# Pooled attention and a top-1 mixture of experts: four instead of two early slots, their tokens turned by way of a DRAM scratch, and one table for all later slots

## The chip, the cores and the metric

The kernel runs on one core of a Trainium2 chip. The metric is device microseconds for one execution. A core has TensorE (PE in the profile: matmuls and transposes), VectorE (DVE), ScalarE (ACT), GpSimd (POOL, which also issues the gathers and scatters) and SyncE (SP, which issues the plain DMAs). Each works through its own instructions in order, and semaphores make them wait for one another.

## The reference

```python
# q, k, v: [8, 8, 576, 64]; attention over keys and values averaged in groups of 8
k_p = k.reshape(B, H, Sp, 8, D).mean(axis=3)
v_p = v.reshape(B, H, Sp, 8, D).mean(axis=3)
scores = scale * np.matmul(q, k_p.transpose(0, 1, 3, 2))
attn = softmax(scores)
x = np.matmul(attn, v_p)                   # as [4608 tokens, 512]
# each token goes to one of 8 experts
logits = x @ w_gate + modality_bias[modality_id]
e_idx = np.argmax(logits, axis=1)
gate_w = probs[np.arange(N), e_idx]        # softmax of the logits, at the chosen expert
for e in range(E):
    mask = e_idx == e
    h = np.maximum(x[mask] @ w1[e], 0.0)   # 512 -> 1024
    out[mask] = gate_w[mask, None] * (h @ w2[e])   # 1024 -> 512
```

## The kernel before

**Two stages.** Attention runs in 20 steps (lines 980 to 1062), each over up to 256 tokens. Its results go to a DRAM buffer `xs`, one row of 528 numbers a token: 512 values, the gate weight in column 512 and eight factors. The expert stage then runs over slots of 256 tokens of one expert (`part`, line 1303). There are 18 full slots of tokens, and a few more are needed because each expert's last slot is only partly filled.

**Slots.** For each slot, GpSimd gathers its rows of `xs` into `xg` (line 144), the tokens are brought from [token, feature] to [feature, token], and split into a high and a low part (`xhl`) for matmuls in fp32r. The first layer is `first_pair` (line 204): two of eight blocks of 128 hidden units at a time, eight matmuls of 512 columns (line 209) and eight of 256 (line 214). Behind them ScalarE copies half of the sums (line 217), VectorE adds the other (line 218), and the results are split again (lines 221 and 223). The second layer is `second` (line 1337), six matmuls a block. `pairs` (line 1377) runs one slot so: the first layer of a pair, then the second layer of the pair before it. At a slot's end `next_pair` starts the first pair of the next slot, for which that slot's `xhl` must be complete, both parts of both tiles of 128 tokens.

**Slot 0** is shorter. Its first layer (`first0`, line 227) runs among the last steps of attention, so that `slot0` (line 1451) has eight calls of `second`, with `next_pair` of slot 1 ahead of the last one.

**Early slots.** Slots 0 to EARLY_SLOTS - 1 hold tokens of the first expert (that of the first token) out of the first half of the tokens alone (T_EARLY tiles), so that they can be listed before attention is done. `early_table` (line 841) makes their index table `gidx0`: VectorE operations on line 868, one for each of 2 x EARLY_SLOTS columns, two on line 870, 18 matmuls (line 860), and five small operations (lines 834 to 838), behind which the gathers are issued. The operations of this table and of the routing of a group of tokens (`route`, line 731) are a list, `drip`. `gap(n)` (line 546) issues up to n of them in the gaps of VectorE's attention work, but stops at a *held* one, which has matmuls. A held one is issued by `release` at the start of a step (line 995), and only if it stood at the head of the list when line 1055 looked, in the step before:

```python
            due = bool(drip) and drip[0] in held        # line 1055, behind hook_2 of a step
```

The early table enters the list in step 11, behind the routing of the second group; the third group's routing enters in step 16, behind the table. Slot 0's tokens are turned by TensorE at the end of step 17 (line 921).

**Two ways to turn tokens.** `x_transposes` (line 167) uses eight matmuls of TensorE (line 173) for a slot's two tiles, a copy of ScalarE (line 175) and a subtraction of VectorE (line 176). Slots from FIRST_BLOCKED = 3 go another way ("blocked"): `blocks_out` (line 1251) has VectorE multiply by the factors into an order of 32 x 32 blocks, and SP writes each tile to a DRAM scratch `scr`; `blocks_in` (line 1266) reads it back in four transfers a tile; `blocks_turn` (line 1276) has VectorE transpose the blocks; `blocks_high` (ScalarE) and `blocks_low` (VectorE) split. `misc` (line 1410) places these: out in the slot before the one before at f = 4 and 5, in two blocks later, turn, high and low in the slot before at f = 2 to 5. Here `f` is the block of the slot in hand.

**Tables for later slots.** After the last group's routing, `late` (line 1212) places counts, bases, expert numbers, and two tables (`table`, line 1132): six columns (slots 2 to 4) in slots 0 and 1, and 44 columns (the rest) in slots 1 and 2. Each has 36 matmuls (line 1142) and three wide VectorE operations (lines 1144 and 1147). Weights are loaded by SP under a condition (`load_w`), only where a slot's expert differs from the one before; after slot 0 the first expert's weights are loaded again without a condition, because the raw tiles had been used otherwise.

Of the kernel before, what the change touches and what calls it, by code (L numbers as in the profile page):

```python
# [25 lines left out]
EARLY_SLOTS = 2  # L26
EXTRA = (128,)
QUAD = 32
FIRST_BLOCKED = 3
# [4 lines left out]
def kernel(  # L34
# [114 lines left out]
    def gather(s, idx, col, xgs, rows=NTOK):  # L149
        for tt in range(2):  # L150
            gather_tile(xgs[(2 * s + tt) % 4], idx, col + tt, rows)
# [52 lines left out]
    def first_pair(f, ab, between=lambda: None, mid=lambda: None):  # L204
# [6 lines left out]
        mid()  # L211
# [27 lines left out]
    with ExitStack() as actx:  # L239
# [601 lines left out]
        def early_table():  # L841
# [31 lines left out]
            ops += [lambda: [gather(s, gidx0, 2 * s, xg, T_EARLY * P) for s in range(EARLY_SLOTS)]]  # L873
# [286 lines left out]
    def row(a):  # L1160
# [9 lines left out]
        lambda: load_regs(EARLY_SLOTS, meta[0:1, 1 + EARLY_SLOTS:2 + EARLY_SLOTS], None),  # L1170
# [26 lines left out]
    for i, r in enumerate(EXTRA):  # L1197
# [13 lines left out]
    first_cols = table(c4, c4 + 6)  # L1211
# [36 lines left out]
    def gate_of(s, tt):  # L1248
        return gc[:, 2 * s + tt:2 * s + tt + 1] if s >= EARLY_SLOTS - 1 else xg[(2 * s + tt) % 4][:, D:D + 1]

    def blocks_out(s, tt):

        x = xg[(2 * s + tt) % 4] if tt < 2 else xe
        to = xg[(2 * s + 2 + tt % 2) % 4][:, 0:D] if s > FIRST_BLOCKED else ye[:, (4 + tt) * D:(5 + tt) * D]
        xp = to.rearrange("p (j k r) -> p j k r", j=NQ, r=QUAD)
        f = x[:, RX:RX + H].rearrange("p (k a o q) -> p k a o q", a=2, o=1, q=1)
        for a in range(2):
            nc.vector.tensor_tensor(
                xp[:, 2 * a:2 * a + 2].rearrange("p j k r -> p k j r"),
                x[:, 0:D].rearrange("p (k a j r) -> p a k j r", k=ND, a=2, j=2)[:, a],  # L1260
                f[:, :, a].to_broadcast([P, ND, 2, QUAD]), op=ALU.mult)
# [4 lines left out]
    def blocks_in(s, tt):  # L1266
        n = len(tts_of(s))
        if tt == 0 and s <= FIRST_BLOCKED + 1:
# [7 lines left out]
    def blocks_turn(s, tt):  # L1276
        if s <= FIRST_BLOCKED + 1:
# [25 lines left out]
    def part(s):  # L1303
# [49 lines left out]
        def renew(f):  # L1353
# [297 lines left out]
```

## Time and profile before

| | |
|---|---|
| median of 3 runs | 593.76 us (591.69 to 594.55) |
| the profiled execution's own time | 590.98 us |
| its span, first to last instruction | 589.3 us |
| TensorE busy | 570.9 us, 97% of the span |
| VectorE, ScalarE, GpSimd busy | 372.7, 273.8, 187.2 us |
| mean granted clock of TensorE | 0.998 |
| DMA | 92.60 MB, mean 157 GB/s |

A row of a timeline has the start in us from the span's start, the time from the first to the last of the instructions that it merges, engine, line, operation, tiles and shapes, and in brackets the idle time of the engine before it and what ended that. The chain of work that ended last has start, length and what. A row of stretches has the stretch, its length, busy time and number of instructions of PE, PEld (weight loads), DVE, ACT and POOL, the granted clock, the DMA engines' busy share and GB/s. SPq and the like is the issuing of DMAs by that engine.

### The profile page before, as it was taken

The page shows a single profiled execution, that of the slowest core. Times are in us where ns is not written, and L with a number is a line of the kernel's source. Part 1 is how long each engine was busy: PE and PEld are TensorE (multiplying, and loading weights), DVE is VectorE, ACT ScalarE, POOL GpSimd, SP SyncE. Part 2 cuts the span into 40 slices and gives each one's busy share as a digit, 9 for nine tenths or more (in the row PEclk, how much of TensorE's full clock was granted, in tenths as well). Part 3 has the DMA queues.
Part 4 walks back from the last instruction along what each step waited for, and adds up shares of the span by engine and source line. Part 5 has one row for each costly group of instructions (what it writes and reads, how often), then busy time and mean ns, then how long its engine had stood idle before and what let it go on. Part 6 is the DMA issues. An engine that isn't in the chain of part 4 may idle for free.

```text
span 589.3 us, 12333 instructions
## 1 busy us (share of the span) xinstructions
PE 570.9 (97%) x3539; PEld 499.6 (85%) x3539; DVE 372.7 (63%) x945; ACT 273.8 (46%) x652; POOL 187.2 (32%) x290
## 2 busy tenths in 40 slices
PE   6999999999999999999999999999999999999995
PEld 5789789988898888888888888888888888888894
DVE  5877898788966766557455446855455487555311
ACT  2767677788552333333333336633333474334210
POOL 7679967765000323112112102112102113212101
PEclk9999999999999999999999999999999999999999
DMA  8999979995311744232232277242234843241101
GB/s 257 306 323 282 360 219 309 304 313 171 103 54 39 263 169 121 79 125 91 82 118 95 86 230 241 91 125 91 87 111 137 255 158 105 91 146 54 38 3 55
DMA packets 83426, 92.60 MB, mean 157 GB/s; under 512 B 17871, under 2 KB 58319, under 8 KB 83344
## 3 DMA queue, kind: packets, MB, share of 16 engines
q1 hardware_dynamic: 77424, 72.24, 39.2%
q0 software_dynamic: 5920, 19.44, 9.9%
q8 instruction: 30, 0.49, 0.4%
q14 instruction: 52, 0.43, 0.2%
HBM read 123.06 MB, written 27.58 MB: 256 GB/s over the span
## 4 chain that ended last, share of the span: by engine, by line
PE 82%; DVE 7%; DMA 5%; ACT 2%; issue 1%; SPq 1%; POOLq 0%; POOL 0%; DVEq 0%; ACTq 0%
PE op L1345 33%; PE hp L209 20%; PE hp L214 10%; PE av L667 4%; PE hp L183 3%; PE sc L603 3%; DMA q<-in_q_dram 3%; PE av L671 2%; DMA v<-in_v_dram 2%; PE pp L632 2%; PE pq L578 2%; PE ph L183 1%; DVE mx L610 1%; DVE hl L141 1%; DMA out_dram<-obw,slw 1%
## 5 line engine op out<-in xcount | busy, mean ns | idle before, releaser
L209 PE MATMUL hp<-xhl,hl 128*128 128x512 f32 x512 | 126.6, 390 | 0.0
L1321 POOL DMA_INDIRECT out_dram<-ob,sidx x34 | 36.8, 1083 | 263.6 <-DVE ob L1315 191.2
L209 PEld LDWEIGHTS hp<-xhl,hl 128*128 128x128 f32 x512 | 96.1, 188 | 19.9
L217 ACT COPY ht<-hp 128x256 f32<-128x256 f32 x128 | 47.3, 373 | 138.7 <-PE hp L214 112.3
L218 DVE TENSOR_TENSOR ht<-ht,hp 128x256 f32<-128x256 f32 x128 | 52.8, 420 | 92.5 <-ACT ht L217 89.4
L1345 PE MATMUL op<-hl,hx 128*128 128x512 f32 x429 | 104.8, 392 | 0.0
L1345 PEld LDWEIGHTS op<-hl,hx 128*128 128x128 f32 x429 | 78.5, 189 | 14.6
L1345 PE MATMUL op<-hl,hh 128*128 128x512 f32 x256 | 79.8, 393 | 0.0
L214 PEld LDWEIGHTS hp<-xhl,hl 128*128 128x128 f32 x512 | 69.8, 191 | 4.9
L214 PE MATMUL hp<-xhl,hl 128*128 128x256 f32 x512 | 71.5, 283 | 0.0
L1345 PEld LDWEIGHTS op<-hl,hh 128*128 128x128 f32 x256 | 46.0, 189 | 7.8
L667 PE MATMUL av<-vw,pt 128*128 128x146 f32 (+1 forms) x320 | 49.2, 293 | 1.4 <-DVE xb L700 1.3
L1345 PE MATMUL op<-hl,hlo 128*128 128x512 f32 x128 | 49.9, 390 | 0.0
L144 POOL DMA_INDIRECT xg<-xs,gidx x36 | 38.6, 1073 | 29.0 <-DMA raw<-in_moe_w_dram 13.8
L667 PEld LDWEIGHTS av<-vw,pt 128*128 128x128 f32 (+1 forms) x320 | 39.6, 180 | 3.4 <-DVE xb L700 1.0
L223 DVE SCALAR_TENSOR_TENSOR hx<-ht,hx 128x256 fp32r<-128x256 f32 x64 | 27.2, 427 | 18.8 <-DVEq L1350 15.7
L223 DVE SCALAR_TENSOR_TENSOR hlo<-ht,hh 128x256 fp32r<-128x256 f32 x64 | 27.1, 425 | 18.5 <-DVEq L1350 15.3
L603 PE MATMUL sc<-kt,qt 128*128 128x144 f32 x256 | 37.4, 289 | 0.6 <-DVE rs L798 0.3
L603 PEld LDWEIGHTS sc<-kt,qt 128*128 128x128 f32 x256 | 33.2, 190 | 1.6 <-DVE rs L798 0.5
L610 DVE TENSOR_REDUCE mx<-sc 128x8 f32<-128x576 f32 (+1 forms) x40 | 27.7, 692 | 7.5 <-PE sc L603 6.9
L671 PE MATMUL av<-vw,pt 128*128 128x146 f32 (+1 forms) x160 | 30.0, 290 | 0.0
L221 ACT ACTIVATE hx<-ht 128x256 fp32r<-128x256 f32 x64 | 26.2, 419 | 7.4 <-DVE ht L218 5.7
(279 smaller groups left out, 907.7 us busy)
## 6 DMA issues: line engine op xcount, KB each, us to landing
raw<-in_moe_w_dram SPq DMA_DIRECT2D x288, 256.0 KB
xs<-xb SPq DMA_DIRECT2D x16, 528.0 KB
scr<-xg SPq DMA_DIRECT2D x29, 256.0 KB
k<-in_k_dram SPq DMA_DIRECT2D x7, 1024.0 KB
v<-in_v_dram SPq DMA_DIRECT2D x7, 1024.0 KB
q<-in_q_dram SPq DMA_DIRECT2D x7, 1024.0 KB
y<-scr SPq DMA_DIRECT2D x108, 64.0 KB
v<-in_v_dram SPq DMA_DIRECT2D x16, 128.0 KB
```

What stands on the lines that cost most here:

```text
L144: nc.gpsimd.indirect_dma_start(out=x, out_offset=None, in_=xs[0:rows, :], in_offset=IndirectOffsetOnAxis(idx[:, col:col + 1].bitcast(U32), 0),
L209: nc.tensor.matmul(hp[g % 2], hl[g][:, 0, d * P:(d + 1) * P], ab[:, d, :, 0:SLOT], start=(d == 0), stop=False)
L214: nc.tensor.matmul(hp[g % 2][:, 0:SLOT], hl[g][:, 1, d * P:(d + 1) * P], ab[:, d, 0, 0:SLOT], start=False, stop=(d == ND - 1))
L217: nc.scalar.copy(hts[g % 2], hp[g % 2][:, SLOT:2 * SLOT])
L218: nc.vector.tensor_add(hts[g % 2], hts[g % 2], hp[g % 2][:, 0:SLOT])
L223: nc.vector.scalar_tensor_tensor(hlo, hts[g % 2], 0.0, hh.bitcast(F32), op0=ALU.max, op1=ALU.subtract)
L603: nc.tensor.matmul(dst, qt[:, i, :], kt[b % NB][:, :, h * SPL:(h + 1) * SPL], start=True, stop=True)
L610: nc.vector.reduce_max(mx, scv, axis=AX.X)
L667: nc.tensor.matmul(av[hs, u, 2 * VC * gg:2 * VC * (gg + 1)], pt[:, c, hs], vw[y][:, c].rearrange("p a x -> p (a x)"), start=(gg == 0), sto ...
L671: nc.tensor.matmul(dst4[hs], pt4[:, hs], v4[y][:, 2 * u:2 * u + 2, :], start=False, stop=True)
L1321: nc.gpsimd.indirect_dma_start(out=out[:, :], out_offset=IndirectOffsetOnAxis(idx.bitcast(U32), 0), in_=ob, in_offset=None, bounds_check=N ...
L1345: nc.tensor.matmul(ot, l[:, ts_], hl[f][:, w, D:2 * D], start=(f == 0 and n == 0), stop=(f == NF - 1 and n == 2))
```

## The change

EARLY_SLOTS goes from 2 to 4 and FIRST_BLOCKED from 3 to 1. So four slots are filled from the first half's tokens, and the early table has eight columns. Slots 1 to 3 (the second to the fourth) go through the scratch as well. For the early ones the factors are 1, and ScalarE copies into block order in place of VectorE's multiplication. Slot 1's tokens are sent out and read back ahead of slot 0's first `second`, and turned and split in slot 0 at f = 3 to 6. `x_transposes` is left for slot 0 and for slots past the full ones. The two later tables become one of 50 columns (NSLOT goes from 27 to 29), with its VectorE work in slot 1 and its matmuls at the start of slot 2; counts and bases move from f = 3 to f = 2 of slot 0. The weights' reload moves from the end of slot 0 to slot 2 and becomes conditional. Gate weights are always kept in `gc`.

```diff
-EARLY_SLOTS = 2
+EARLY_SLOTS = 4
-FIRST_BLOCKED = 3
+FIRST_BLOCKED = 1
...
-    first_cols = table(c4, c4 + 6)
+    t = table(c4, NCOL, 4)
     late = {
         (0, 0): [lr[9], lr[7], lr[11], lr[8]],
         (0, 1): [lr[10]],
-        (0, 3): [counts, lr[12]] + [fn for pair in zip(bases, lr[13:20]) for fn in pair] + lr[20:25],
-        (0, 4): experts,
-        (0, 5): lr[25:] + columns,
-        (0, 6): first_cols[:3],
-        (1, 0): first_cols[3:] + changes,
+        (0, 2): [counts, lr[12]] + [fn for pair in zip(bases, lr[13:20]) for fn in pair] + [lr[20]],
+        (0, 6): lr[21:24],
+        (0, 7): lr[24:27],
+        (1, 0): lr[27:],
+        (1, 2): experts,
+        (1, 3): columns,
+        (1, 4): changes,
+        (1, 5): t[0:1],
+        (1, 6): t[1:2],
+        (1, 7): t[2:3],
+        (2, 0): t[3:5],
+        (2, 1): t[5:7],
+        (2, 2): t[7:],
     }
...
-    t = table(c4 + 6, NCOL, 4)
-    for i, at_ in enumerate(((1, 3), (1, 7), (2, 1), (2, 3), (2, 4), (2, 5), (2, 6))):
-        late[at_] = t[i:i + 1]
-    late[2, 7] = t[7:]
...
-        to = xg[(2 * s + 2 + tt % 2) % 4][:, 0:D] if s > FIRST_BLOCKED else ye[:, (4 + tt) * D:(5 + tt) * D]
+        to = xg[(2 * s + 2 + tt % 2) % 4][:, 0:D]
...
+            if s < EARLY_SLOTS:
+                nc.scalar.copy(xo, xi)
+            else:
+                nc.vector.tensor_tensor(xo, xi, f[:, :, a].to_broadcast([P, ND, 2, QUAD]), op=ALU.mult)
...
-                if nxt2 and s + 2 > EARLY_SLOTS:
+                if nxt2 and s + 2 == EARLY_SLOTS:
+                    new_raw(f)
+                if nxt2 and s + 2 >= EARLY_SLOTS:
                     load_w(s + 2, f)
...
-                    turn = g == NF - 2 and not blocked(s + 1)
-                    first_pair(g, tokens_of(s), pop, (lambda: x_transposes(s + 1, xg)) if turn else (lambda: None))
+                    first_pair(g, tokens_of(s), pop)
...
-            if f == (3 if s < EARLY_SLOTS else 2) and blocked(s + 2):
-                gather(s + 2, gidx, 2 * (s + 2), xg)
+            if f == 2 and blocked(s + 2):
+                gather(s + 2, xg)
...
                 for tt in tts_of(s + 1):
-                    if f == 4 + tt:
+                    at_ = f - tt - (0 if s else 1)
+                    if at_ == 4:
                         blocks_low(s + 1, tt)
...
                 second(f)
-                renew(f)
-                if f == 4:
-                    x_transposes(s + 1, xg)
                 do_late(s, f)
-            for f in range(NF):
-                new_raw(f)
-                load_w(EARLY_SLOTS, f)
+                misc(f, [])
...
+    for tt in range(2):
+        keep_gate(0, tt, nc.gpsimd)
+        blocks_out(1, tt)
+    for tt in range(2):
+        blocks_in(1, tt)
     for s in range(NSTAT - 1):
         parts[s][0](tail)
```

More of the change, by code (lines that the diff above doesn't have):

```diff
@@ L147, in gather_tile, with gather @@
             bounds_check=rows - 1, oob_is_err=False)
-    def gather(s, idx, col, xgs, rows=NTOK):
+    def gather(s, xgs):
         for tt in range(2):
-            gather_tile(xgs[(2 * s + tt) % 4], idx, col + tt, rows)
+            gather_tile(xgs[(2 * s + tt) % 4], gidx0 if s < EARLY_SLOTS else gidx, 2 * s + tt,
+                        T_EARLY * P if s < EARLY_SLOTS else NTOK)
     def scale_tile(x):
@@ L202, in first_wide, with first_pair @@
         nc.vector.scalar_tensor_tensor(hlo, t, 0.0, hh.bitcast(F32), op0=ALU.max, op1=ALU.subtract)
-    def first_pair(f, ab, between=lambda: None, mid=lambda: None):
+    def first_pair(f, ab, between=lambda: None):
         fs = (f, f + 1)
@@ L210, in first_pair @@
                                  start=(d == 0), stop=False)
-        mid()
         for g in fs:
@@ L872, in early_table @@
             ops += finish_table(lambda: psm["t"], C, gidx0, sidx0, "t0")
-            ops += [lambda: [gather(s, gidx0, 2 * s, xg, T_EARLY * P) for s in range(EARLY_SLOTS)]]
+            ops += [lambda: [gather(s, xg) for s in range(2)]]
             return ops
@@ L1257, in blocks_out @@
         for a in range(2):
[L1258 to L1261, printed above, removed]
+            xo = xp[:, 2 * a:2 * a + 2].rearrange("p j k r -> p k j r")
+            xi = x[:, 0:D].rearrange("p (k a j r) -> p a k j r", k=ND, a=2, j=2)[:, a]
+            if s < EARLY_SLOTS:
+                nc.scalar.copy(xo, xi)
+            else:
+                nc.vector.tensor_tensor(xo, xi, f[:, :, a].to_broadcast([P, ND, 2, QUAD]), op=ALU.mult)
         if tt < 2:
@@ L1267, in blocks_in @@
         n = len(tts_of(s))
-        if tt == 0 and s <= FIRST_BLOCKED + 1:
+        if tt == 0 and s <= EARLY_SLOTS:
             ys[s] = ye[:, 0:n * D].rearrange("p (t u x) -> p t u x", t=n, u=NQ)
@@ L1276, in blocks_turn @@
     def blocks_turn(s, tt):
-        if s <= FIRST_BLOCKED + 1:
+        if s <= EARLY_SLOTS:
             yt = ye[:, (2 + tt) * D:(3 + tt) * D].rearrange("p (k x) -> p k x", k=ND)
@@ L1414, in misc @@
                 slot_flag(s + 2)
-            if f == 0:
+            if f == 0 and s + 2 >= EARLY_SLOTS:
                 slot_regs(s + 2)
-            if f == 0 and s == EARLY_SLOTS - 1:
-                for tt in range(2):
-                    keep_gate(s, tt, nc.gpsimd)
-            if s == 1 and f == 2:
-                gather(s + 1, gidx, 2 * (s + 1), xg)
-            if f == 4 and s + 1 >= EARLY_SLOTS and not blocked(s + 1):
-                scale(s + 1, xg)
-                for tt in range(2):
-                    keep_gate(s + 1, tt, nc.gpsimd)
-            if f == (2 if blocked(s + 1) else 4):
+            if f == 2:
                 while later:
                     later.pop(0)()
-            if f == (3 if s < EARLY_SLOTS else 2) and blocked(s + 2):
-                gather(s + 2, gidx, 2 * (s + 2), xg)
+            if f == 2 and blocked(s + 2):
+                gather(s + 2, xg)
                 if s + 2 == NSTAT - 1:
@@ L1436, in misc @@
                 for tt in tts_of(s + 1):
-                    if f == 4 + tt:
+                    at_ = f - tt - (0 if s else 1)
+                    if at_ == 4:
                         blocks_low(s + 1, tt)
-                    if f == 3 + tt:
+                    if at_ == 3:
                         blocks_high(s + 1, tt)
-                    if f == 2 + tt:
+                    if at_ == 2:
                         blocks_turn(s + 1, tt)
@@ L1480, in run @@
                 if f == CUT and nxt:
-                    gather(s + 1, gidx, 2 * (s + 1), xg)
+                    gather(s + 1, xg)
                 if f:
```

5 lines of the change are left out of this document (2 added, 3 removed).

## The prediction

> **What bounds the kernel now.** I read the page's first lines first, then the busy time by stretch, then the chain of work that ended last between 175 and 275 us, then the timelines of the single engines from 130 to 262 us.
>
> ```profile
> PE 570.9 (97%) x3539; PEld 499.6 (85%) x3539; DVE 372.7 (63%) x945; ACT 273.8 (46%) x652; POOL 187.2 (32%) x290
> ...
> PE 82%; DVE 7%; DMA 5%; ACT 2%; issue 1%; SPq 1%; POOLq 0%; POOL 0%; DVEq 0%; ACTq 0%
> ```
>
> TensorE is busy for 97% of the span and is 82% of the chain. So an edit pays only if it takes instructions from TensorE, and it costs whenever it makes TensorE wait. The stretches (columns: from:to, length, then busy time and count of each engine, granted clock, DMA share, GB/s) say the same of the stage that changes:
>
> ```profile
> 181.00:194.80 13.80, 13.80 (x79) 11.39 (x78) 11.53 (x48) 2.10 (x5) 0.95 (x5) 1.00 0.17 47
> ...
> 262.40:284.50 22.10, 22.10 (x115) 18.90 (x114) 13.37 (x40) 8.08 (x19) 4.08 (x4) 1.00 0.31 99
> ```
>
> Slot 0 (first row) and a plain later slot (second row) have no idle TensorE at all, at full clock. A plain slot is 22.1 us, so one of its four pair steps is 5.5 us. Slot 0 is only 13.8 us long, because its first layer was done during attention. Whatever must be made ready within slot 0 has half the usual time.
>
> **What TensorE is spared.** The chain (start, length, what) between slots 0 and 2:
>
> ```profile
> 181.02 5.56 PE op L1345 x24
> ...
> 188.37 0.87 PE xt L173 x8
> ...
> 192.05 1.84 PE hp L209 x8
> ...
> 196.24 0.90 PE ptab L1142 x36
> 197.14 1.93 PE hp L209 x8
> ...
> 202.77 1.81 PE hp L209 x8
> ...
> 210.10 0.87 PE xt L173 x8
> ...
> 224.34 0.37 PE ptab L1142 x9
> 224.71 1.45 PE op L1345 x6
> ...
> 235.36 0.37 PE ptab L1142 x9
> ```
>
> The transposes of slot 1's tokens (188.37) and slot 2's (210.10) go: 0.87 us each. The six-column table goes: 0.90, and the 0.12 by which the group after it is longer (1.93 against 1.81). The four pieces of the big table (224.34 is the first, 235.36 the last) stay, with 100 columns instead of 88: nine matmuls of 88 take 0.37, nine of 12 take 0.90/4 = 0.225, so 12 more columns add 0.023 a piece, 0.09 in all. They now come in one place; each of four places cost the matmuls behind it 0.06 (six take 1.45, where 5.56/4 is 1.39), so three times that, 0.18, goes. After the start of slot 1's first layer (192.05) this is 0.87 + 0.90 + 0.12 + 0.18 - 0.09 = 2.0 us saved. Before it the first 0.87 goes too, but there the question is when the tokens are ready.
>
> Edits that cost nothing: the 16 weight loads after slot 0 become conditional ones in slot 2, skipped because slot 4 has the same expert; TensorE waits for none of them now. With the reference's own inputs the first expert has 1,114 tokens in the first half, so four slots are full and 19 slots are used, before and after; longer register tables for slots that never run touch nothing. SP's four gate stores now stand behind ten transfers of slot 1's blocks; only the gather of slot 4, in slot 2, needs them. The checks for changed weights leave slot 1; they are not on TensorE's path.
>
> **The early table.** It is dealt out between attention's VectorE steps (line 546), and its matmuls go out only at the start of a step, if they are at the head of the list when line 1055 looks.
>
> ```profile
> 134.22 0.70 DVE L868 SCALAR_TENSOR_TENSOR b<-rh,s 128x18 bf16<-128x18 f32 x4
> ...
> 135.51 0.29 DVE L870 TENSOR_TENSOR b<-b,idw 128x72 bf16<-128x72 bf16 x2
> ...
> 139.65 0.75 DVE L610 TENSOR_REDUCE mx<-sc 128x8 f32<-128x576 f32 x1
> ...
> 141.33 0.16 DVE L836 TENSOR_SCALAR gidx<-t0ix 128x4 int32<-128x4 f32 x1
> ...
> 142.55 1.19 DVE L749 TENSOR_REDUCE lgr<-lg 128x72 f32<-128x576 f32 x1
> ...
> 147.18 0.27 DVE L781 TENSOR_REDUCE dc<-oh 128x8 f32<-128x72 bf16 x1
> ...
> 149.64 0.45 DVE L610 TENSOR_REDUCE mx<-sc 128x4 f32<-128x288 f32 x1
> ```
>
> Step 15 has ten places ahead of that look (2 in s_dve, 4 in x_dve, 2, and 2 in the next s_dve), and before there are exactly ten operations behind the count: two on adjv, two for s0, four on line 868, two on 870. With eight on line 868 there are fourteen, the table's matmuls are not at the head, and they slip from step 16 to step 17. So the indices, which followed the reduction at 139.65, will follow the one at 149.64. Step 16 is lighter, as the ten routing operations from 142.55 to 147.18 slip behind the table as well: about 3 us of VectorE, of which I count 1.5, since the next group also waits for TensorE and ScalarE. The reduction is then at about 148.1, and the gather 1.6 after it, at 149.7 (before it was 2.1, from 139.65 to 141.78; the reduction and the subtraction behind it, 0.75 each there, are the 0.45 kind here).
>
> ```profile
> 141.78 1.25 POOL L144 DMA_INDIRECT xg<-xs,gidx  x1 [4.77 <-DVE t0lo L837]
> DMA to landing us min/median/max: 3.4/3.6/7.8
> 150.56 0.60 PE L173 MATMUL xt<-ident,xg 128*128 128x128 f32 x4
> 151.89 0.77 PE L667 MATMUL av<-vw,pt 128*128 128x146 f32 x4 [0.72 <-DVE xb L700]
> ...
> 158.63 1.25 PE L603 MATMUL sc<-kt,qt 128*128 128x144 f32 x8 [0.28 <-DVE rs L798]
> 163.28 0.66 PE L632 MATMUL pp<-ident,pe 128*128 128x128 f32 x4 [0.54 <-DVE h L187]
> ```
>
> A gather at 149.7 lands at 153.3. TensorE turns slot 0's first tile at 150.56, so it waits 2.7 us; the waits of 0.72, 0.28 and 0.54 behind it take up 1.5. Left: **+1.2 us** (from 0, if VectorE gains all 3 us, to +2.7, if nothing is absorbed).
>
> **Slot 1's tokens.** They are now copied by ScalarE, written to the scratch, read back, turned by VectorE, split, all within slot 0.
>
> ```profile
> 183.99 0.26 ACT L757 ACTIVATE ex<-lgr 128x72 f32<-128x72 f32 x1 [2.48 <-DVE lgr L756]
> 196.29 0.75 ACT L221 ACTIVATE hh<-ht 128x256 fp32r<-128x256 f32 x2 [1.04 <-DVE ht L218]
> 256.87 1.69 SPq L1264 DMA_DIRECT2D scr<-xg  x2
> 260.46 3.66 SPq L1274 DMA_DIRECT2D y<-scr  x8
> 257.50:258.40 0.90, 0.90 (x7) 0.78 (x6) 0.90 (x4) 0.67 (x2) 0.00 (x0) 1.00 0.74 278
> 260.90:265.50 4.60, 4.60 (x25) 3.96 (x24) 1.80 (x7) 1.58 (x4) 0.00 (x0) 1.00 0.40 114
> 220.79 3.68 SPq L1274 DMA_DIRECT2D ye<-scr x8
> 228.41 0.71 DVE L1282 STREAM_TRANSPOSE ye<-ye 128x512 f32<-128x512 f32 x1 [2.31 <-DMA ye<-scr]
> 226.13 0.62 ACT L1286 CAST xhl<-ye 128x512 fp32r<-128x512 f32 x1 [1.86 <-DVE ye L1282]
> 231.28 0.69 DVE L1291 TENSOR_TENSOR xhl<-ye,xhl 128x512 fp32r<-128x512 f32 x1
> ```
>
> ScalarE's copies stand behind the exponential of the last route, which ends at 184.25. Two copies of that size take 0.75 to 0.8, so the first tile is written from 185.1. The write issued at 256.87 moved its bytes from 257.50 to 258.40; I take 2.1 until SP may read (at most 3.6, to the first read at 260.46). So reading starts at 187.2. Eight reads issued from 260.46 moved bytes until 265.50, 5.1 us later: the second tile is there at 192.3. Turn 0.71, high part 0.62, low part 0.69 and three hand-overs of 0.1: 194.6. The low part also stands behind a gate copy that waits for slot 2's gather, and three operations on arow of 0.2: I take 195.2. TensorE starts slot 1 at 192.05 now and could at 191.2 without the transposes; instead it waits 4 us, and **+3.2 us** is left (bounds: +2.2 with nothing behind; +5.7 if the reads take as long as those from 220.79, which ended 7.6 us later, at 228.41, 2.5 more than 5.1). The count's matmul now goes out one second() earlier and may wait for cum; that lies inside the 4 us.
>
> Slots 2 and 3 make the same trip under the 22.1 us of matmuls of slot 1 and slot 2, as later slots do now, at no cost to TensorE; without that cover it would be slot 1's 4 us again. A gain beyond the saved instructions is excluded throughout, since TensorE has no idle time here to give back.
>
> **Sum.** +1.2 + 3.2 - 2.0 = +2.4 us. The profiled execution took 590.98 us (span 589.3), so 593.4 of its kind; the median of the three runs is 593.76 (591.69 to 594.55), and 596.2 is my forecast. A measurement of this kernel can tell about 0.5% from no change, 3.0 us.
>
> **Rivals.**
> - *All hidden.* If the gather still arrives in time and the blocks are back before 191.2, only the savings stay: -2.0 - 0.9 = -2.9, 590.9. For it: VectorE has its own slack in step 16. Against it: the trip adds up from rows without waits. 0.08.
> - *The trip is held up, slower than before.* Slot 2's gather starts when the first write has landed, and moves its bytes among the reads; the reads from 220.79, beside a scatter, were 2.5 us late. It decides from 0.6 us of delay on (2.4 + 0.6 = 3.0). Fully it gives +4.9, 598.7. 0.17.
> - *VectorE becomes the bound of slot 1.* The big table's passes take 2.0 us each (the row below, 1.79 for 1,584 elements, now 1,800), and two fall into one pair step beside 13.37/4 = 3.3 us of standing work: 7.4 against 5.5. If the steps before run late too (experts, columns, changes), TensorE waits for the 1.9 us: +4.3, 598.1. 0.12.
>
> ```profile
> 202.13 1.79 DVE L1144 TENSOR_TENSOR bsel<-iota_f,col 128x1584 bf16<-128x1584 f32 x1
> ```
>
> - *The clock falls in the new wait.* No stretch shows less than 1.00 and TensorE never waits 1 us in the expert stage, so the trace cannot tell. If the pair behind the wait ran at half clock it would take 2.8 us longer (1.84 + 0.95): +5.2, 599.0. 0.08. [...]
>
> **How the numbers follow.** The forecast's own case has 0.55; its bounds, 0 + 2.2 - 2.0 = +0.2 and +2.7 + 3.2 - 2.0 = +3.9, put 0.42 of it within 0.5% and 0.13 above. The held-up trip gives 0.16 slower and 0.01 same; VectorE 0.08 and 0.04; the clock 0.07 and 0.01; all hidden 0.06 faster and 0.02 same. Together: faster 0.06, same 0.50, slower 0.44. The range goes from 592.5 (the lower bound +0.2 less the spread of the runs, 1.5) to 600.5 (late reads, +1.2 + 5.7 - 2.0 = +4.9, and 1.8 for the spread).
>
> **What would show it.** Right: line 144's first gather near 150 instead of 141.78, and TensorE waiting 2 to 3 us at line 173 for it; a wait of 3 to 5 us at line 209 for xhl on VectorE near 195; eight transposes at line 173 and 36 matmuls at line 1142; the stretch from slot 1's start to slot 3's 2 us shorter. Wrong: no wait at line 209 (then the trip is faster than its rows), a gather still at 142 (then the slip is not there), waits of TensorE for line 218 in slot 1 (VectorE), a granted clock under 1.00 behind the wait.

## The result

The changed kernel takes 600.44 us in the median (598.87 to 601.75, 6 runs); the kernel before, beside it, 592.17 (591.60 to 594.55, 6 runs). The ratio is 1.0148, with a 95% interval of 1.0118 to 1.0178. So the change makes the kernel slower by about 1.5%, where 596.2 us was forecast, a change too small to be told from none. The profiled execution took 598.87 us, with a span of 597.1 us, 7.8 more than the 589.3 of before.

From the page of the kernel after: TensorE's and VectorE's busy time, the granted clock in forty slices, and the shares of the chain.

```profile
PE 569.4 (95%) x3487; PEld 496.0 (83%) x3487; DVE 375.4 (63%) x945; ACT 278.4 (47%) x664; POOL 182.8 (31%) x286
PEclk9999999999999799999999999999999999999999
PE 81%; DMA 6%; DVE 6%; issue 2%; ACT 2%; SPq 1%; POOLq 0%; POOL 0%; DVEq 0%; ACTq 0%
```

TensorE has 52 instructions less (3487 against 3539) and is busy for 1.5 us less, yet the span is longer: TensorE waits. And one slice of the clock, the fourteenth, shows a 7. The chain of the kernel after has the place, and the saved work behind it:

```profile
187.57 0.17 PE pcnt L1102
...
188.00 5.66 PE op L1349 x24
193.67 5.70 issue
199.37 3.75 PE hp L210 x8
203.12 1.05 PE hp L214 x8
...
227.63 1.64 PE ptab L1142 x36
```

The change shifted the lines: 210 was 209, 1349 was 1345. In front of slot 1's first layer TensorE does nothing for 5.70 us, and its first eight matmuls then take 3.75 us instead of 1.84. The transposes between 188 and 210 us are gone, and the table has one place. The stretch from slot 1's start to slot 3's, first before, then after (stretch, length, busy time and count of PE, PEld, DVE, ACT, POOL, granted clock, DMA share, GB/s):

```profile
191.88:238.40 46.52, 46.52 (x299) 39.53 (x298) 31.25 (x82) 15.61 (x38) 15.30 (x14) 1.00 0.55 183
```
```profile
199.37:245.74 46.37, 46.37 (x255) 39.33 (x255) 32.12 (x80) 17.17 (x42) 8.22 (x8) 0.96 0.31 101
```

It is 0.15 us shorter, although the clock was 0.96 in it. Here is the whole account of the profiled executions, after against before:

| where | read from | us |
|---|---|---|
| attention, to slot 0's start | 180.86 to 182.57 | +1.7 |
| slot 0, to slot 1's start | 11.02 to 16.80 | +5.8 |
| slow first matmuls of slot 1 | line 210's group, 3.75 for 1.8, and its neighbour | +2.0 |
| the work saved up to slot 3 | 46.37 - 2.0 against 46.52 | -2.2 |
| from slot 3 on | the rest | +0.5 |
| sum | | +7.8 |

The trip of slot 1's tokens in the kernel after, by its rows in order of time (start, time, engine, line):

```profile
185.92 1.31 ACT L1263 COPY xg<-xg 128x256 f32<-128x256 f32 x4
186.64 0.93 SPq L1268 DMA_DIRECT2D scr<-xg  x2
188.85 0.32 SPq L1278 DMA_DIRECT2D ye<-scr  x1
189.23 1.41 SPq L1278 DMA_DIRECT2D ye<-scr  x1
188.85 4.64 SPq L1278 DMA_DIRECT2D ye<-scr  x8
189.44 1.06 POOL L144 DMA_INDIRECT xg<-xs,gidx  x1 [1.49 <-DMA scr<-xg]
190.81 1.00 POOL L144 DMA_INDIRECT xg<-xs,gidx  x1 [0.30 <-issue]
195.90 1.40 DVE L1286 STREAM_TRANSPOSE ye<-ye 128x512 f32<-128x512 f32 x2 [6.11 <-DMA xs<-gate]
```

From the first copy to the first read's issue it is 2.93 us (forecast: 187.2 - 184.25 = 2.95). From there to the second tile's turn it is 7.75 us: the two turns take 0.7 each, so the second starts at 196.60. The forecast was 5.1. From the second turn to slot 1's start it is 2.77 us (forecast 2.9). The whole surprise of this trip, 2.65 us, thus lies among the eight reads. Two things stand out there: slot 2's gather runs between them, and the second read takes 1.41 us to issue, where the forecast's rows had 3.66 for eight. All eight take 4.64 now. (The last row names a gate store as what ended VectorE's wait; the experiment that moves these stores takes that up.)

What came out as forecast is seen in attention:

```profile
137.28 0.37 DVE L870 TENSOR_TENSOR b<-b,idw 128x144 bf16<-128x144 bf16 x2
...
148.23 0.45 DVE L610 TENSOR_REDUCE mx<-sc 128x4 f32<-128x288 f32 x1
149.31 0.16 DVE L836 TENSOR_SCALAR gidx<-t0ix 128x8 int32<-128x8 f32 x1
149.77 1.26 POOL L144 DMA_INDIRECT xg<-xs,gidx  x1 [5.60 <-DVE t0lo L837]
153.63 0.63 PE L174 MATMUL xt<-ident,xg 128*128 128x128 f32 x4 [2.88 <-DMA xg<-xs,gidx]
165.01 0.65 PE L632 MATMUL pp<-ident,pe 128*128 128x128 f32 x4 [1.01 <-DVE h L188]
```

The early table slipped by a step: the first gather starts at 149.77 (forecast 149.7, before 141.78), and TensorE waits 2.88 us for it (forecast 2.7). Of that, 1.7 reached slot 0's start in this execution (forecast 1.2).

The clock around slot 1's start, in the kernel after:

```profile
193.65:196.20 2.55, 0.00 (x1) 0.00 (x0) 0.30 (x1) 0.00 (x0) 0.00 (x0) 1.00 0.78 176
196.20:196.50 0.30, 0.00 (x0) 0.00 (x0) 0.30 (x1) 0.00 (x0) 0.00 (x0) 0.84 0.70 6
196.50:199.37 2.87, 0.00 (x1) 0.04 (x1) 2.68 (x9) 2.37 (x6) 0.00 (x0) 0.50 0.18 64
199.37:203.10 3.73, 3.73 (x9) 2.96 (x10) 0.00 (x0) 0.00 (x0) 0.00 (x0) 0.50 0.49 164
203.10:203.40 0.30, 0.30 (x4) 0.30 (x3) 0.00 (x0) 0.00 (x0) 0.00 (x0) 0.78 0.68 183
203.40:205.50 2.10, 2.10 (x14) 1.84 (x13) 1.27 (x3) 1.58 (x4) 0.00 (x0) 1.00 0.36 95
```

It falls to 0.50 within the wait, at about 196.4 (0.84 over 0.30 us is full clock for 0.2 of them), and is back at about 203.2. The matmuls of 199.37 to 203.10 ran at half clock.

### The profile page after: what moved, and what is told of

The parts are those of the page before. It is cut to its first block, busy times and chain, and to the rows that moved or that the text cites. A ratio compares the mean times of both kernels' runs of the same rounds, so it can differ in the third digit from the quotient of the medians.

```text
span 597.1 us, 11997 instructions
## 1 busy us (share of the span) xinstructions
PE 569.4 (95%) x3487; PEld 496.0 (83%) x3487; DVE 375.4 (63%) x945; ACT 278.4 (47%) x664; POOL 182.8 (31%) x286
## 4 chain that ended last, share of the span: by engine, by line
PE 81%; DMA 6%; DVE 6%; issue 2%; ACT 2%; SPq 1%; POOLq 0%; POOL 0%; DVEq 0%; ACTq 0%
PE op L1349 32%; PE hp L210 20%; PE hp L214 10%; PE av L667 4%; PE hp L184 3%; PE sc L603 3%; DMA q<-in_q_dram 3%; PE av L671 2%; PE pp L632 2%; DMA v<-in_v_dram 2%; PE pq L578 1%; PE ph L184 1%; DMA out_dram<-obw,slw 1%; DVE mx L610 1%; DMA raw<-in_moe_w_dram 1%
## 5 line engine op out<-in xcount | busy, mean ns | idle before, releaser
L210 PE MATMUL hp<-xhl,hl 128*128 128x512 f32 x512 | 130.1, 396 | 5.7 <-issue 5.7
L1325 POOL DMA_INDIRECT out_dram<-ob,sidx x34 | 35.5, 1044 | 286.9 <-DVE ob L1319 214.1
```

The costliest lines, as they stand in the source:

```text
L210: nc.tensor.matmul(hp[g % 2], hl[g][:, 0, d * P:(d + 1) * P], ab[:, d, :, 0:SLOT], start=(d == 0), stop=False)
L1325: nc.gpsimd.indirect_dma_start(out=out[:, :], out_offset=IndirectOffsetOnAxis(idx.bitcast(U32), 0), in_=ob, in_offset=None, bounds_check=N ...
```

## Experiments

The theory after the result: three costs, each by itself. The slipped early table costs 1.7 us. Slot 1's trip costs 5.8, of which the gather and one read's issue are what the forecast lacked. The clock that falls in the wait costs 2.0. Rivals: SyncE's gate stores hold up the reads; the clock is not the reason for the slow matmuls; the trip is late because it starts late, not because it is held up; something else in the change (VectorE in slot 1, the one table) takes the time. Ratios are to the kernel before, on the same chip. In the experiments up to the eighth the lines are those of the kernel after, or a few off.

**Keep TensorE busy in the wait.** Spare matmuls fill the wait and do nothing else.

```diff
                 if f == NF - 1:
+                    tf = ps_tr.tile([P, P], F32, tag="tr", name="tfill")
+                    for _ in range(90):
+                        nc.tensor.matmul(tf, iota_b, iota_b, start=True, stop=True)
                     next_pair()
```

> The changed kernel with 90 spare matmuls (128 x 128, bf16, results unused) on TensorE between the seventh second() of slot 0 and the first layer of slot 1, so that TensorE is busy while it waits for slot 1's tokens. If the eight matmuls at line 210 took 3.75 us instead of 1.81 because the clock had fallen in the 5.7 us wait, they take about 1.8 us again, no stretch shows a clock under 0.97 there, and the run is about 2 us faster than the changed kernel (1.011 against before). If they were slow for another reason (the tokens' tiles being written, PSUM), they stay near 3.7 us and the time stays at 1.015.

Measured: 597.88 us, 1.0117 (1.0098 to 1.0136). TensorE's rows of this run:

```profile
200.35 2.06 PE L210 MATMUL hp<-xhl,hl 128*128 128x512 f32 x8 [0.54 <-PE tfill L1453]
```

Slot 1 starts no earlier behind slot 0's start (16.70 us, 16.80 unaltered), but its first eight matmuls take 2.06 instead of 3.75 us, and the granted clock stays at 1.00. From slot 1's start to the end the profiled execution takes 395.25 us, against 397.73 in the kernel after and 397.90 in the next run, where the clock falls. So the clock is shown to be the reason for the slow matmuls, and useless work in the wait gains 2 to 2.5 us behind it. The ratio is 0.3% lower, but that by itself shows nothing: the intervals overlap, and the next run, with wait and clock as before, has nearly the same ratio.

**Gate stores out of the trip's way.** The last of the gate's operations, with its stores, goes from slot 0 to slot 1.

```diff
-        (0, 1): [lr[10]],
...
+        (1, 1): [lr[10]],
```

> The changed kernel with the four stores of the last gate weights moved from slot 0 to slot 1, behind the block transfers of slot 2 in SP's queue. If these stores (4-byte pieces) delay the reading back of slot 1's blocks, the turns on VectorE start near 193.5 instead of 195.9 and TensorE waits about 3.5 us at line 210 (1.011 against before). If it is the gather of slot 2, nothing moves: the turns stay near 196, wait 5.7 us, 1.015.

Measured: 598.52 us, 1.0124 (1.0107 to 1.0141). The first read is issued at 188.23, the second tile turned at 196.00, 7.77 us later, as before (7.75). TensorE waits 5.5 us, and line 210 takes 3.75. The gate stores are not the cause. The ratio is 0.24% under that of the result although nothing in the trip changed; differences of that size between ratios say nothing here, and the rows decide.

**Hold slot 2's gather until the reads have landed.** GpSimd copies four columns of each landed tile ahead of the gather; slot 2's blocks go out two places later.

```diff
             if f == 2 and blocked(s + 2):
+                if s == 0:
+                    for tt in range(2):
+                        nc.gpsimd.tensor_copy(hold[:, 4 * tt:4 * tt + 4], ys[1][:, tt, :, 0])
                 gather(s + 2, xg)
...
-                    at_ = f + NF * (s + 2 - q) - tt - 4
+                    at_ = f + NF * (s + 2 - q) - tt - (6 if q == 2 else 4)
```

> The changed kernel with slot 2's gather held by GpSimd until slot 1's blocks are back (GpSimd copies eight columns of them first), and slot 2's trip two blocks later. If the gather among the reads makes them late, eight reads take 3.7 us to issue again, the turns start near 193.5 instead of 195.9, TensorE waits 3 to 4 us at line 210 and the clock falls less or not at all: 2 to 4 us faster than the changed kernel (1.008 to 1.011). If the gate stores are the cause, no change: turns near 196, 1.015.

Measured: 598.02 us, 1.0122 (1.0097 to 1.0146). SyncE's issues and TensorE's row:

```profile
189.77 0.32 SPq L1279 DMA_DIRECT2D ye<-scr  x1
190.15 1.44 SPq L1279 DMA_DIRECT2D ye<-scr  x1
```
```profile
198.41 3.43 PE L210 MATMUL hp<-xhl,hl 128*128 128x512 f32 x8 [3.84 <-issue]
```

The second turn is at 195.94, 6.17 us behind the first read's issue instead of 7.75. So the gather among the reads costs 1.6 us of the 2.65. (That slot 2's blocks go out later has no part in it: unaltered, their writes are issued at 198.03, behind both turns.) The second read still takes 1.4 us to issue. After a wait of 3.84 us the clock falls too (3.43 for line 210).

**The last call of the second layer ahead of the next pair.** TensorE does slot 0's last six matmuls before it waits, not behind.

```diff
+                second(f)
                 if f == NF - 1:
                     next_pair()
-                second(f)
```

> The changed kernel with the last second() of slot 0 ahead of slot 1's first layer instead of behind it, so that 1.4 us of TensorE's work lies inside the wait. The tokens come when they come: the wait falls from 5.7 to about 4.3 us and slot 1 starts at the same time, so 1.4 us are gained; if the clock then falls less, up to 2 us more (1.009 to 1.013). If slot 1's second layer then waits for the sums of the pair (ScalarE and VectorE need about 1.8 us), part of the 1.4 us is lost again.

Measured: 597.55 us, 1.0126 (1.0094 to 1.0159). The wait falls to 3.77 us. That alone only moves work, but line 210's group takes 2.79 instead of 3.75:

```profile
195.73:199.50 3.77, 0.01 (x1) 0.04 (x1) 3.21 (x9) 2.36 (x6) 0.00 (x0) 1.00 0.37 79
199.50:202.30 2.80, 2.80 (x10) 2.25 (x11) 0.00 (x0) 0.00 (x0) 0.00 (x0) 0.70 0.48 162
202.30:204.00 1.70, 1.70 (x8) 1.40 (x7) 0.41 (x1) 0.37 (x1) 0.00 (x0) 0.50 0.48 125
```

The clock is full for the whole wait and falls behind it, while TensorE works again.

**The changed kernel again**, as the mark for the three that follow on the same chip.

> The changed kernel unaltered, beside the next three on one chip, as the measure for them. Every theory expects 1.015 against before, a wait of 5.7 us at line 210 and the clock at half behind it.

Measured: 600.92 us, 1.0151 (1.0125 to 1.0176), as in the result. In its profiled execution it is 8.23 us from the first read's issue to the second turn (190.64 to 198.87), TensorE waits 5.99 us, and line 210 takes 3.75.

**The early table in time.** Four of the waiting operations are issued ahead of step 15's look at the list.

```diff
+            if n == 15:
+                gap(4)
```

> The changed kernel with four more places for the early table's operations in step 15 of attention, ahead of the look at the head of the list. If the slip of the table from step 16 to step 17 costs what the trace shows, the first gather starts near 142 instead of 149.8, the wait of 2.9 us at line 174 is gone and slot 0 starts 1.2 to 1.7 us earlier: 1.012 against before. If the four operations in front of the subtraction of the scores cost as much as they save, the start of slot 0 does not move and the ratio stays at 1.015. The wait in slot 0 stays as it is in both.

Measured: 1.0111 (1.0078 to 1.0145), 599.37 us in the median; one of its six runs took 2,806 us and is not in the ratio. The first gather is at 142.83 (149.77 unaltered):

```profile
142.83 1.26 POOL L144 DMA_INDIRECT xg<-xs,gidx  x1 [5.50 <-DVE t0lo L837]
```

TensorE does not wait at line 174 any more. Slot 0's wait (6.1 us) and line 210's 3.75 stay. Against 1.0151, that is 0.4% or 2.4 us, where the account has 1.7; the intervals overlap. The slip is a cost by itself, and the execution of the account shows only part of it, since there the clock stayed full behind the wait in attention. With the gather held, a wait of 2.78 us at the same place is followed by half clock (first the kernel after, then the gather held):

```profile
153.60:157.00 3.40, 3.37 (x29) 3.40 (x30) 1.77 (x9) 1.85 (x5) 1.03 (x2) 1.00 0.67 203
```
```profile
153.50:157.00 3.50, 3.50 (x18) 3.49 (x16) 0.97 (x4) 0.66 (x2) 1.00 (x1) 0.51 0.63 179
```

Of the nine profiled executions with the slip, in the result and the experiments, four show this fall, each for 3.41 us: with the spare matmuls, with the gather held, in the changed kernel again and in the first try at undisturbed reads. Slot 0 starts at 182.85 on the average of the nine (181.72 to 184.37), and at 180.92 in the six without the slip (180.28 to 181.77). So the slip is worth some 1.9 us.

**Slot 1 by TensorE, the rest as changed.** The trip of slot 1 is undone alone; early slots, the one table and the slip stay.

```diff
-FIRST_BLOCKED = 1
+FIRST_BLOCKED = 2
...
+                if f == 4:
+                    x_transposes(s + 1, xg)
...
-        blocks_out(1, tt)
-    for tt in range(2):
-        blocks_in(1, tt)
+        keep_gate(1, tt, nc.gpsimd)
```

> The changed kernel with slot 1's tokens turned by TensorE in slot 0, as before the change (eight transposes, 0.9 us); slots 2 and 3 still go through the scratch, the early table and the one later table stay. If the trip inside slot 0 and the clock behind it are the loss, TensorE does not wait at line 210, the clock stays at 1.00, and 5.7 + 2.0 - 0.9 = 6.8 us are gained on the changed kernel: 1.003 against before. If the wait moves to slot 2's tokens, whose blocks are now out in slot 0 as well, it shows at the start of slot 2 and the gain is smaller.

Measured: 592.60 us, 1.0016 (0.9996 to 1.0035). Nothing waits at line 210, and the slip's 2.7 us at line 174 stay. The gain is a little larger than expected (1.003); the expectation took 0.9 us off for the transposes, which the 5.8 us of the account already allow for. Slot 1's trip, with the clock that it lets fall, is thus worth 1.35% or 8.0 us, about the 5.8 + 2.0 of the account. What else is in the change (VectorE, the table) does no harm.

**Both undone**: the last edit, the early table in time, and the counts back at f = 3 of slot 0.

```diff
-        (0, 2): [counts, lr[12]] + [fn for pair in zip(bases, lr[13:20]) for fn in pair] + [lr[20]],
+        (0, 3): [counts, lr[12]] + [fn for pair in zip(bases, lr[13:20]) for fn in pair] + [lr[20]],
```

> The changed kernel with slot 1's tokens turned by TensorE, the early table in time and the counts back at f = 3 of slot 0. If attention's slip (1.7 us), the trip with the clock (6.8 us) and the wait for the counts (0.7 us) are all that was lost, only the savings are left, about 2 us: 0.996 to 0.998 against before. If the new order costs elsewhere (VectorE in slot 1), it stays at 1.000 or above.

Measured: 589.83 us, 0.9978 (0.9959 to 0.9997); taken again, further down, 0.9974 (0.9955 to 0.9994). This version is faster than the kernel before too, by some 1.4 us. The savings left in it (the one table, slot 2's transposes) were forecast at 2.0 us; that they are what is seen is inferred. With the counts back, a wait of 0.65 us of TensorE for `cum` in slot 0 is gone, which in the kernel after lies inside the wait for slot 1.

**Start the trip early.** In the same kernel, but with the trip, slot 1's four copies and two writes go out in attention, at the step before the last two; the reads stay where they were. (Early table in time, counts at f = 3.)

```diff
+        def send_slot1():
+            for tt in range(2):
+                to = xg[tt][:, 0:D]
...
+                nc.sync.dma_start(scr[1, tt * P:(tt + 1) * P, :], to)
+        at(hook_3, N - 2, send_slot1)
...
-        blocks_out(1, tt)
+        keep_gate(1, tt, nc.vector)
```

> The changed kernel, with three edits: four of the waiting operations are issued ahead of step 15's look (so the early table is not late), the counts go back from f = 2 to f = 3 of slot 0, and slot 1's four ScalarE copies and its two writes to the scratch are issued in attention, at the step before the last two, instead of behind the last route. Nothing is left out. If the trip is late because it starts behind the last route's exponential, the first read of slot 1 is issued 2.5 to 5 us earlier than 188.2, the wait at line 210 is 2 us or less, the granted clock there stays at 1.00, and the time is about that of the kernel in which TensorE turns slot 1's tokens, or up to 1 us under it because eight transposes are spared: 0.996 to 0.999 of the kernel before. If the reads themselves wait (the memory that they fill is only free once the last users of attention are done, near 187), the first read stays near 188, the wait of 5 us and the fall of the clock stay, and the ratio is 1.009 to 1.012.

Beside it ran the version without the trip:

> The changed kernel with slot 1's tokens turned by TensorE, four of the waiting operations issued ahead of step 15's look, and the counts back at f = 3 of slot 0: the same kernel as the one measured at 0.998 of the kernel before, taken again beside the one whose trip starts early, so that the two are compared on one chip. Nothing is left out. Expected again 0.996 to 1.000 under every theory, with no wait over 1 us at line 210. If the trip's late start was the cause, the other kernel is equal to this one or up to 1 us faster; if the reads wait for their memory, it is 6 to 8 us slower.

Measured: 595.23 us, 1.0060 (1.0037 to 1.0082), against 589.97 us, 0.9974 (0.9955 to 0.9994). Neither expectation of the first holds. Its rows, SyncE, VectorE, TensorE:

```profile
184.65 4.80 SPq L1290 DMA_DIRECT2D ye<-scr  x8
...
186.44 1.58 SPq L1290 DMA_DIRECT2D ye<-scr  x1
192.62 0.71 DVE L1298 STREAM_TRANSPOSE ye<-ye 128x512 f32<-128x512 f32 x1 [2.31 <-DMA ye<-scr]
195.22 3.75 PE L211 MATMUL hp<-xhl,hl 128*128 128x512 f32 x8 [4.62 <-issue]
```

The reads start at 184.65, 4.2 us earlier than unaltered, of which 2.3 are slot 0's own earlier start (180.28 instead of 182.57), with the table in time. What they read was written from 163.38 on, but they wait for VectorE's `oh` of the last route, whose memory they fill (in the queue's own waits: 1.1 us for it, behind 3.0 for a store). But the trip is no shorter for it: from the first read to the second turn it takes 7.97 us, TensorE waits 4.6, and the clock falls. A late start is only part of the cost; the reads, again beside slot 2's gather (185.82 and 187.21), are held up here too. And the read whose issue is long is now the fifth, at 186.44.

That was a hint. In each of these runs, a 16 KB transfer of queue 8, of kind "instruction", begins within 0.25 us of the start of the long issue (in 189.2 to 189.3 in the kernel after, 190.1 to 190.2 with the gather held, 186.2 to 186.3 here). And in the kernel after and here alike TensorE is then about 36 matmuls into slot 0. The kernel before has the same, on a gate store: the transfer begins at 187.2 to 187.3, and of SyncE's four stores there, which take 0.55, 0.58 and 0.63 us otherwise, one takes 1.38:

```profile
187.41 1.38 SPq L787 DMA_DIRECT2D xs<-gate  x1
```

**The reads undisturbed, first try.** Gather held, as above, and SyncE's instructions numbered differently by eight spare loads of 32 bytes in attention, on the theory that SyncE's own program is loaded.

```diff
+        idle8 = cp.tile([1, 64], F32, name="idle8")
+        def spare_loads():
+            for i in range(8):
+                nc.sync.dma_start(idle8[:, 8 * i:8 * i + 8], w_gate[i:i + 1, :])
+        at(hook_3, N - 4, spare_loads)
```

> The changed kernel with the gather of slot 2 held until slot 1's reads have landed (as in the run with the gather held), and with eight spare loads of 32 bytes on SyncE, in attention, so that SyncE's instructions are numbered differently and the 16 KB instruction transfer that began 0.05 us ahead of the second read's issue falls elsewhere. The spare loads are added work and nothing is left out. If the two causes together make up the lateness, the issue of the eight reads takes 3.7 instead of 4.65 us, the time from the first read's issue to the second turn is 5.1 to 5.4 us (7.75 unaltered, 6.17 with the gather held alone), the wait at line 210 is 2.6 to 3.2 us, line 210's eight matmuls take under 2.8 us, and the ratio to the kernel before is 1.005 to 1.010. If the instruction transfer is only a coincidence, the second read takes 1.4 us again, and the time is that of the gather held alone: 6.2 us and 1.010 to 1.013.

Measured: 598.02 us, 1.0120 (1.0098 to 1.0142). The second read is as long as ever, the transfer begins at 189.0, again 6.7 us behind slot 0's start, and the trip takes 6.08 us, as with the gather held alone (6.17):

```profile
188.98 1.34 SPq L1285 DMA_DIRECT2D ye<-scr  x1
```

The same two edits in the kernel with the early trip:

> The kernel with the early trip (copies and writes in attention, the early table in time, counts at f = 3 of slot 0), with the gather of slot 2 held and the eight spare loads as in the run beside it. The spare loads are added work and nothing is left out. If the reads, then undisturbed, take 5.1 to 5.4 us from the first issue near 184.7, the second tile is turned near 190, slot 1 starts near 192.3, the wait at line 210 is 1 to 2 us with the clock at 1.00, and the ratio is 0.995 to 0.999. If the reads take 8 us as with the early trip alone whatever is beside them, the wait stays at 4.5 us and the ratio at 1.004 to 1.008.

Measured: 592.64 us, 1.0027 (1.0008 to 1.0045), outside both expected ranges; 6.15 us from first read to second turn, with the fifth read long again. The transfer begins with the long read here too (187.4). Since it does not move when SyncE's instructions do, it is not SyncE's program that is loaded: that theory falls. TensorE waits 2.69 us, and behind that too the clock falls, to 0.50 for 3.41 us:

```profile
191.64:193.80 2.16, 0.00 (x0) 0.00 (x0) 1.95 (x6) 0.62 (x1) 1.38 (x2) 1.00 0.27 2
193.80:194.00 0.20, 0.00 (x0) 0.00 (x0) 0.20 (x1) 0.00 (x0) 0.20 (x1) 0.85 0.00 0
194.00:194.33 0.33, 0.00 (x0) 0.03 (x1) 0.23 (x1) 0.00 (x0) 0.10 (x1) 0.50 0.00 0
194.33:197.20 2.87, 2.87 (x7) 2.29 (x8) 0.15 (x1) 0.67 (x2) 1.01 (x1) 0.50 0.66 178
197.20:197.50 0.30, 0.30 (x3) 0.24 (x2) 0.00 (x0) 0.04 (x1) 0.00 (x0) 0.74 0.26 99
```

**The reads undisturbed, second try.** The spare loads go; TensorE's instructions are moved instead, by 24 more filling matmuls at the start of attention, where TensorE waits.

```diff
-        fill(14)
+        fill(32)
...
-        fill(8)
+        fill(14)
```

> The changed kernel with the gather of slot 2 held until slot 1's reads have landed, and with 24 more of TensorE's filling matmuls (128x128, bf16) at the very start of attention, where TensorE waits for 0.96 and 0.23 us. They are added work, and nothing is left out. In all runs so far the 16 KB instruction transfer of queue 8 began when TensorE was 36 to 38 matmuls into slot 0, wherever SyncE then was. If it is TensorE's own program that is loaded, 24 matmuls more ahead move it to TensorE's 12th to 14th of slot 0, about 185.5 us, where SyncE issues nothing: then no read takes over 0.5 us to issue, the eight take 3.7 us, the time from the first read's issue to the second turn is 5.0 to 5.4 us, the wait at line 210 is 2.5 to 3 us, and the ratio is 1.006 to 1.011. If it isn't TensorE's, the second read takes 1.4 us again and the trip 6.1 us, as in the run with the spare loads.

Measured: 596.87 us, 1.0099 (1.0075 to 1.0124). Reads, second turn and TensorE:

```profile
188.64 3.64 SPq L1279 DMA_DIRECT2D ye<-scr  x8
193.82 0.71 DVE L1287 STREAM_TRANSPOSE ye<-ye 128x512 f32<-128x512 f32 x1 [1.11 <-DMA ye<-scr]
196.29 3.44 PE L210 MATMUL hp<-xhl,hl 128*128 128x512 f32 x8 [2.84 <-issue]
```

The instruction transfer is at 181.3 now (farther than the expected 185.5), no read is long, and the trip takes 5.18 us: the forecast's 5.1. With the gather held alone it took 6.17, so the long issue costs 1.0. What was missing is accounted for: 1.6 + 1.0 of 2.65. TensorE still waits 2.84 us, and the clock falls (3.44).

And with the early trip:

> The kernel with the early trip (copies and writes in attention, the early table in time, counts at f = 3 of slot 0), with the gather of slot 2 held and the 24 filling matmuls at the start as in the run beside it. They are added work, and nothing is left out. If the instruction transfer moves with TensorE's program, it falls near 183.4 us, ahead of the reads, all of them take 0.43 us to issue, the second tile is turned 5.0 to 5.4 us after the first read's issue, near 190, the wait at line 210 is 0.5 to 1.8 us, the clock stays at 1.00, and the ratio is 0.995 to 1.000. If not, one read takes 1.4 us, the wait is 2.7 us, the clock falls, and the ratio stays at 1.001 to 1.005.

Measured: 592.07 us, 1.0017 (1.0004 to 1.0030), just above the expected range.

```profile
185.07 3.65 SPq L1291 DMA_DIRECT2D ye<-scr  x8
190.29 0.71 DVE L1299 STREAM_TRANSPOSE ye<-ye 128x512 f32<-128x512 f32 x1 [0.76 <-DMA ye<-scr]
192.76 2.08 PE L211 MATMUL hp<-xhl,hl 128*128 128x512 f32 x8 [1.74 <-issue]
...
586.60 0.98 POOL L1631 DMA_INDIRECT out_dram<-obl,sl  x1 [4.66 <-DMA out_dram<-obw,slw]
```

The trip takes 5.22 us, the wait is 1.74, and the clock stays. By the pair that starts at 541.63 before, and at 540.77 here, TensorE is 0.9 us ahead of the kernel before; but the last scatter of this execution waits 4.66 us for the one before it (2.68 for `obl` before), so its span is 590.8 against 589.3. Whether the last scatters are late in all its runs was not tried and stays open. With the gather, the long issue and the fall of the clock gone, a wait of 1.74 us is left, and the kernel is still not faster than the one in which TensorE turns slot 1's tokens (0.9974).

## Why the prediction was wrong

- *What bounds the kernel.* Right. Time came only from TensorE's waits and from its clock.
- *The savings, -2.0.* Right: -2.2 up to slot 3. The one table takes 1.64 us (forecast 4 x 0.37 + 0.09 = 1.57).
- *The early table, +1.2.* Right in its mechanism and its times (gather at 149.77, wait 2.88), and somewhat small: +1.7, and +1.9 on the average of the executions. The waits behind it were not all taken up; one of them grew from 0.54 to 1.01. And behind the wait the clock fell in four of nine executions; the prediction asked that only of slot 1's wait.
- *Slot 1's trip, +3.2: the step that failed.* "Eight reads issued from 260.46 moved bytes until 265.50, 5.1 us later" was taken for reads in slot 0. Beside slot 2's gather and an instruction transfer they needed 7.75, and the term came to 5.8. The rows before and behind the reads were right to 0.2 us, and with both disturbances gone the trip takes 5.18: the estimate was right for reads that are alone, and these are not. The nearest row, the reads from 220.79, "beside a scatter", had 2.5 us more and was kept as an upper bound, +5.7, and as the held-up rival with 0.17. It was the better row, since the change itself puts a gather there, but that its 7.6 comes so near to 7.75 is in part luck: its eight reads took 3.68 us to issue, without a long one. The gather explains 1.6 of the 2.65. The other 1.0, the long issue, was not on the list, though the kernel before shows one at 187.41. Over all profiled executions the three cases lie apart: 7.42 to 8.37 us from first read to second turn with gather and long issue (seven), 6.08 to 6.17 with the long issue alone (three), 5.18 and 5.22 with neither.
- *The clock, a rival with 0.08, taken apart from the others.* It came true together with the held-up trip, at +2.0 instead of the +2.8 forecast, and the two belong together: in slot 0 the clock fell behind each of the ten waits of 2.69 us or more and stayed at 1.00 behind the one of 1.74. The half clock was the rival's assumption, which no row of the prediction shows; the runs show 0.50, for 6.83 us in the kernel after. Two separate chances, 0.17 and 0.08, hid that their joint case was the likely one once the wait was 4 us or more. The wait forecast was 4 us; in the experiments the clock falls with waits of 2.69, 2.84, 3.72, 3.77 and 3.84 us too. In these it is low for 3.41 us, of which TensorE works for 2.93 or more, so that half of that, 1.5 to 1.7 us, is lost. So even the forecast's own case should have held most of these 2.0 us.
- *VectorE the bound of slot 1, all hidden.* Neither happened; nothing waits for VectorE in slot 1.

By its own terms the sum was +2.4; +0.5 for the table, +2.6 for the reads and +2.0 for the clock make it +7.5, of the +7.8 measured between the two spans.

The prediction left open whether the clock falls in a wait of 4 us. The traces answer it for the waits that occurred in slot 0: it fell behind those of 2.69, 2.84, 3.72, 3.77 and 3.84 us, behind five of 4.62 to 6.11, and not behind the one of 1.74. The low times are 3.41 us (193.94 to 197.35 in the early trip with spare loads) and 6.83 us (196.41 to 203.23 in the kernel after), one and two times the same length. The stretches at full clock are whole multiples of it too: 187.73 us ahead of that fall in the kernel after and 392.53 behind it, 55 and 115 times 3.413; in the kernel before 576.85, 169 times, up to 587.14, where the clock goes to 0.50 behind TensorE's last work. With the gather held the falls and rises come at 153.56, 156.97, 197.93 and 201.34, which is 1, 13 and 14 times 3.413 us behind the first.

If the kernel after is divided into intervals of 3.413 us from its fall at 196.41, TensorE was busy for 0.66 us in the interval that ends with the fall, for 0.45 in the next, behind which the clock stayed low, and for 3.41 in the third, behind which it came back. In all others between 10 and 576 us it was busy for 1.81 us or more, and the clock stayed at 1.00. The wait of 2.88 us in attention fell across two of these, busy for 2.14 and 1.81 us. In the kernel before TensorE was busy for 2.25 us or more in each, and the clock stayed too. The time ahead of a fall was not all idle: in the early trip with spare loads TensorE stopped at 191.64, 2.3 us ahead of the fall, so that it worked for up to 1.11 us in the 3.41 us before that. And the changed kernel again has a fall behind 1.91 us of work (from 67.15), more than the 1.81 behind which it stayed in the kernel after. So what sets the clock is not shown, nor whether every wait of 4 us would have had the fall; none of the ten of 2.69 us or more in slot 0 escaped it.

## What to carry to other kernels

A transfer that is moved to a new place takes the duration of that place (here 7.75 us beside the gather and the long issue, 5.18 without them): price it by the row that ran beside the same neighbours, and look at what the change itself will start there. A wait of TensorE can cost more than its length: behind waits of 2.69 to 3.84 us the clock was at 0.50 for 3.41 us here, which cost 1.5 to 1.7, and behind 5.70 us for 6.83, which cost 2.0; add that to the same case, not to a separate one. One profiled execution shows whether the clock fell in that one; look at several. And where a stage is too short for a trip through DRAM, the engine that is the bottleneck may still be the cheaper one: eight transposes cost 0.87 us here, the trip that replaced them 5.8 and 2.0 more.

## What the runs showed of the hardware

- In the kernel after the clock was full for 187.73 us, at 0.50 for 6.83 and full for 392.53: 55, 2 and 115 times 3.413 us. In the kernel before it was full for 576.85 us, 169 times that. It fell to 0.50 behind all ten waits of 2.69 to 6.11 us in slot 0, behind four of nine waits of 2.7 to 2.9 us in attention, and not behind 1.74 us in slot 0. In the kernel after TensorE had been busy for 0.66 us in the 3.41 us ahead of the fall. With a wait of 3.77 us the clock fell 1.1 us after TensorE worked again. It came back after 3.86 us of work in the kernel after (199.37 to 203.23) and after 2.93 with the gather held (198.41 to 201.34). What sets it is not shown.
- Where a 16 KB transfer of kind "instruction" began within 0.25 us of the start of a DMA issue of SyncE, that issue was longer: 1.34 to 1.58 us for a read that takes 0.43 otherwise (1.41 in the kernel after, 1.44 with the gather held, 1.58 in the early trip, 1.34 with the spare loads), and 1.38 for a gate store of the kernel before that takes 0.55 otherwise. The transfer moved from 189.2 to 181.3 when 24 matmuls were added to TensorE's work, and was at 189.0 when eight loads were added to SyncE's. Why the two go together isn't shown.
- With a GpSimd gather of two tiles beside the eight reads of 64 KB the second tile's turn came 7.75 us behind the first read's issue, and 6.17 with the gather held: 1.6 us (1.3 to 2.3 over the executions).
